# Threshold attention and feed-forward on one core: the last two score tiles of five head pairs take their threshold from a DMA add instead of VectorE

## The chip, the cores and the metric

One Trainium2 chip, one core. The metric is the device time of one execution in microseconds. The engines are named as in the profile: PE is TensorE (PEld its weight loads), DVE is VectorE, ACT is ScalarE, POOL is GpSimd, SP is SyncE. Every engine takes its instructions from its own queue in order and waits on semaphores; SP, ACT and POOL also issue DMAs.

## The reference

```python
# q, k, v: (8, 8, 576, 64) float32; tau scalar; w_in (512, 2048), w_out (2048, 512)
scores = scale * np.matmul(q, k.transpose(0, 1, 3, 2))
thresh = np.max(scores, axis=-1, keepdims=True) - tau
scores = np.where(scores >= thresh, scores, -1000000000.0)
scores = scores - np.max(scores, axis=-1, keepdims=True)
attn = np.exp(scores)
attn = attn / (np.sum(attn, axis=-1, keepdims=True) + 1e-09)
attn_out = np.matmul(attn, v)
x = attn_out.transpose(0, 2, 1, 3).reshape(4608, 512)
h = x @ w_in
out = (h * (1.0 / (1.0 + np.exp(-1.702 * h)))) @ w_out
```

## The kernel before, in words

The heads are worked in 32 pairs, four pairs (numbers 0 to 3) being the first batch. A pair's scores are held transposed, keys on partitions: `scores` makes nine groups of 64 keys of both heads (four matmuls each, two trace instructions per float32 matmul), and `keep` (ACT, L588) copies each group from PSUM into SBUF. Two groups form a tile of 128x1152; there are four such tiles and a short one of 128x576, numbered t = 0 to 4.

The threshold of a query is the maximum over keys less tau. DVE reduces each tile (`in_groups`, L594) and then over tiles (`over_tiles`, L603); ACT crosses the partition halves (`cross_max`, L613) and DVE joins them (`over_halves`, L620). For the pairs in `BY_DMA` (1, 3, 4, 5, 6) the result is turned (`turn_rows`, L627), written to a row in DRAM (`row_out`, L643) and read back over all partitions into a tile `mb` (`row_in`, L652), both issued on POOL. The others spread it by a DVE transpose (`spread_max`, L631). Then, tile by tile, DVE subtracts the threshold (`sub`, L658), ACT multiplies what is negative by a steep factor (`mask`, L664) and takes the exponential (`exps`, L668). PE multiplies by the values (L679, `pv`) and, for pairs 0 to 3, by ones for the sums (L679, `den`); `place_x` (L783) scales the product into the feed-forward input.

The weights arrive as 32 pieces that ACT and DVE convert: `cv_power` (L494), `cv_power2` (L498) and `cv_round` (L512) on ACT, `cv_low`, `cv_whole` and `cv_end` (L526) on DVE. The first two feed-forward blocks are plain: `mm1_0` (L838), `tanh`, `gelu_0`, then `mm2` (L820). The later blocks use seven products in place of eight (`product1`, L908; `product`, L1230), for which sums of weight quarters are made by accumulating DMAs on POOL (`t_plus`, L954; `w_plus`, L877). From pair 6 on, the scores of a pair are interleaved on PE with the products of an earlier one.

The order of all this is fixed when the program is built. Each step is a `task` with an engine, a planned cost and a rank; the tables `EARLY` (pairs 0 to 3), `SECOND` (4 to 7), `LATER`, `CV`, `W_RANK` and `L_RANK` are offsets to the ranks. `run_in_order` plays the planned costs, and on each engine emits the ready task of lowest rank. So a change of one cost or rank can change the order on every engine. A `transfer` stands for a DMA in that plan.

Of the kernel before, what the change touches and what calls it, by code (L numbers as in the profile page):

```python
# [17 lines left out]
ALU = mybir.AluOpType  # L18
# [14 lines left out]
def kernel(  # L33
# [81 lines left out]
    flat = [const.tile([P, 32], FP32, name=f"flat{j}") for j in range(2)]  # L115
# [15 lines left out]
    for x in ("raw0", "raw1", "qkT0", "qkT1", "mb"):  # L131
# [3 lines left out]


    EARLY = {
        "cross_max": -48.44,
        "exps": 8.27,
        "in_groups": -20.58,  # L140
        "keep": -91.91,
        "load_qk": -140.68,
        "load_v": -22.28,
        "mask": 10.76,
        "one_row": -86.85,
        "over_halves": -24.87,
        "over_tiles": -88.47,
        "place_x": -38.02,
        "row_in": 3.21,
        "row_out": -7.31,  # L150
        "scores_run": -131.23,
        "spread_max": 29.73,
        "spread_sums": 7.58,
        "sub": -0.95,
        "sums_by_pe": 0.48,
        "turn_in": -85.72,
        "turn_rows": -3.66,
        "turned": -73.29,
        "values": 4.21,
    }  # L160
    SECOND = {
        "cross_max": 21.33,
        "cross_sums": 28.0,
        "exps": -7.59,
        "in_groups": 89.35,
        "keep": 7.69,
        "load_qk": -3.13,
        "load_v": 156.87,
        "mask": 62.12,
        "over_halves": -25.79,  # L170
        "over_tiles": 12.47,
        "place_x": -6.25,
        "prep": 141.1,
        "row_in": 11.9,
        "row_out": 159.53,
        "scores_run": -65.52,
        "spread_max": 4.94,
        "sub": 100.98,
        "sums_in": 1.57,
        "sums_out": 102.83,  # L180
        "turn_rows": -12.68,
        "turn_sums": -7.39,
        "values": -29.52,
    }
    LATER = {
        "cross_max": 26.13,
# [17 lines left out]
        "values": 4.3,  # L204
    }
    CV = {
        "cv_end": 0.86,
        "cv_low": 87.73,
        "cv_power": 34.31,
        "cv_power2": 17.48,  # L210
        "cv_round": -2.96,
        "cv_whole": 74.25,
        "load_w": -29.8,
    }

    LAG = {"PE": 0.26, "DVE": 0.18, "ACT": 0.22, "POOL": 0.18, "SP": 0.1}
# [5 lines left out]
    def task(engine, cost, rank, f, *a, after=(), take=(), give=(), lag=None):  # L222
        if lag is None:
            lag = LAG[engine]
        if rank != FIRST and rank < LAST and f not in (first_act, tau_terms, run_up, stay_warm):
            biases = EARLY if a[0] < NPAIR else SECOND if a[0] < 2 * NPAIR else LATER
            rank += CV[f.__name__] if f.__name__ in CV else biases.get(f.__name__, 0.0)
        tasks.append((engine, cost, rank, f, a, [x for x in after if x is not None],
                      take, give, lag))
        return len(tasks) - 1  # L230
# [9 lines left out]
    def transfer(by, time, a, kind=0, give=(), lag=1.7):  # L240
        return task(by, time, FIRST, moved, kind, after=[a], give=give, lag=lag)
# [102 lines left out]
    BY_POOL = {}  # L344
# [63 lines left out]
    def own(n, *pools):  # L408
        return tuple(x + "_apart" for x in pools) if n in APART else pools
# [122 lines left out]
    mats, sT, stats, mbs, rows, pss = {}, {}, {}, {}, {}, {}  # L532
# [92 lines left out]
    def turn_rows(n):  # L625

        nc.vector.transpose(out=flat[1], in_=flat[0])  # L627

    def spread_max(n):
        mb = home(n, "mb")  # L630
# [16 lines left out]

    def row_in(n):
        mb = home(n, "mb")
        row = rows.pop(n)  # L650
        for c in range(2):
            row_queue(n).dma_start(out=mb[ts(c, KT)], in_=row[c : c + 1].to_broadcast([KT, S]))  # L652
        mbs[n] = mb

    def sub(n, t):
        s = sT[n, t].rearrange("p u h s -> p u (h s)")
        engine = nc.gpsimd if t in BY_POOL.get(n, ()) else nc.vector
        engine.tensor_tensor(  # L658
            out=s, in0=s, in1=mbs[n].unsqueeze(1).to_broadcast(list(s.shape)), op=ALU.subtract
        )  # L660

    def mask(n, t):
# [607 lines left out]
    for x in other:  # L1270
# [4 lines left out]
        out=eye, in_=eye, compare_op=ALU.not_equal, fill=1.0, base=0, pattern=[[-1, P]],  # L1275
# [3 lines left out]
        out=tau_b, in_=bass.AP(tensor=tau.tensor, offset=tau.offset, ap=[[0, P], [1, 1]])  # L1279
# [36 lines left out]


    SUMS_BY_PE = (0, 1, 2, 3)
    BY_DMA = (1, *range(3, SINGLE))
    SUMS_BY_DMA = range(4, NP)  # L1320
    LEAD = 6
# [4 lines left out]
    FFU = 1.727  # L1326
    T_RANK = FIRST

    W_RANK = (-72.29, -7.42, 1.49, 46.38, 3.78, 10.04)
    W_TIME = 1.8  # L1330
    WARM = 22
    ROUND_BY_ACT = range(n_in)
# [2 lines left out]
    for i in range(len(pieces)):  # L1335
        y = 0 if i < NDC else 2 if i < n_in else 4
        n = NDC if i < NDC else n_in - NDC if i < n_in else n_in
# [28 lines left out]
    placed, spread, ffn = {}, {}, []  # L1366
# [478 lines left out]
            next_blk += 1  # L1845

    crossed = {"max": [], "sums": []}
    L_RANK = (-39.87, -74.91, 155.66, -21.93, -34.74, 174.67, -5.56, -9.93, 5.49, 3.95, 23.52, -15.1, 43.37, 150.16, 100.05, 1.56, -41.98, 6.75, 20.12, -0.89, 1.38, 148.42, -40.7, -50.66)

    def load_rank(n, which):  # L1850
        return L_RANK[3 * n + which] if 3 * n < len(L_RANK) else 0.0
# [16 lines left out]
    for n in range(NP):  # L1868
        gate = per_pair * (n - LEAD)
        assert gate < len(ffn) or gate <= 0  # L1870
        after = [ffn[gate]] if gate >= 0 and ffn else []
        r = float(n)

        slow = 1.1 if n < 2 * NPAIR else 1.0
        rq = ("POOL", 1.4, "DMW", 2.2) if n in ROWS_BY_POOL else ("SP", 1.0, "DMS", 1.7)
        flow = 2.9 if n in (0, 1, 4) else 0.0
        by_sp = n not in ROWS_BY_POOL
# [31 lines left out]
        mx, copies = [], []  # L1909
# [18 lines left out]
        if n >= JOINT:  # L1928

            a = None  # L1930
            for t in range(NKT + 1):
                js = range(2 * t, min(2 * t + 2, NK))
                m = ahead(n)
                w = task(
                    "PE", 0.485 * len(js), r, values, m, [t],
                    after=exped[m] + [loaded[m], pq, pk] + after if t == 0 else [a],
# [6 lines left out]
                a = w  # L1943
                for j in js:
                    w = task(
                        "PE", 0.485, r, scores_run, n, [j], after=[a], take=("psA",),
                        give=own(n, "qkT0", "qkT1") if j == NK - 1 else (),
# [3 lines left out]
                    a = w  # L1951
                if t == NKT:
                    valued(m, w)
        else:
            for js in [range(x, x + 3) for x in range(0, NK, 3)] if n >= WHOLE else [[x] for x in range(NK)]:
# [3 lines left out]
                a = task(  # L1959
                    "PE", 0.484 * slow * len(js), r, scores_run, n, js, after=[pq, pk] + after,  # L1960
                    take=("psA",) * len(js) + new,
                    give=own(n, "qkT0", "qkT1") if js[-1] == NK - 1 else (),
                )
                after = [a]
                for j in js:
                    copied(n, r, j, a)
        a = task("DVE", 0.41, r, over_tiles, n, ALU.max, after=mx)
        quick = n in BY_DMA
        a = task(
            "ACT", 0.45 if quick else 0.85, r, cross_max, n, after=[a, tau_done] + crossed["max"],  # L1970
        )
        a = task("DVE", 0.24, r, over_halves, n, after=[a], take=("row",) if quick else ())
        crossed["max"] = [a]
        if n in BY_DMA:
            a = task("DVE", 0.14, r, turn_rows, n, after=[a])
            a = transfer(rq[2], 0.3 + 0.4 * by_sp, task(rq[0], 0.65 * rq[1], r, row_out, n, after=[a]), lag=1.7 - 0.4 * by_sp + flow)
            spread[n] = task(rq[0], 1.1 * rq[1], r, row_in, n, after=[a], take=own(n, "mb"))
            m = transfer(rq[2], 1.1, spread[n], 0 if by_sp else 1, give=("row",), lag=rq[3] + flow)
        else:
            m = task("DVE", 0.78, r, spread_max, n, after=[a], take=own(n, "mb"))  # L1980
        spread.setdefault(n, m)
        ws, subs = [], [(m, None)]
        for t in range(NKT + 1):
            tail = t == NKT
            pool = t in BY_POOL.get(n, ())
            a = task(
                "POOL" if pool else "DVE", (1.45 if pool else 0.68) if tail else 2.7 if pool else 1.3,
                r, sub, n, t, after=[y for y, x in subs if tail or x in (None, pool)],
                give=own(n, "mb") if tail else (),
            )  # L1990
            subs.append((a, pool))
            a = task("ACT", 0.58 if tail else 1.08, r, mask, n, t, after=[a])
            ws.append(task("ACT", 0.77 if tail else 1.25, r, exps, n, t, after=[a]))
        loaded[n] = lv
# [87 lines left out]
```

## Time and profile before

| | us |
|---|---|
| median of 3 runs | 1248.26 (1247.51 to 1250.88) |
| the profiled execution | 1251.82 |
| its span, first to last instruction | 1250.0 |
| outside the span | 1.8 |
| PE busy | 1222.6 (98%) |
| DVE busy | 1085.7 (87%) |
| ACT busy | 827.7 (66%) |
| POOL busy | 32.6 (3%) |

A group line of the profile gives line, engine, operation, output and input with their shapes, the count, then busy time in us and the mean length of one in ns, and last the idle time of the engine just before them with what ended it. A line of the order in time gives start and length in us, and in brackets the idle time before it. Line numbers are those of the kernel before.

### The profile page before, as it was taken

The page shows a single profiled execution, that of the slowest core. Times are in us where ns is not written, and L with a number is a line of the kernel's source. Part 1 is how long each engine was busy: PE and PEld are TensorE (multiplying, and loading weights), DVE is VectorE, ACT ScalarE, POOL GpSimd, SP SyncE. Part 2 cuts the span into 40 slices and gives each one's busy share as a digit, 9 for nine tenths or more (in the row PEclk, how much of TensorE's full clock was granted, in tenths as well). Part 3 has the DMA queues.
Part 4 walks back from the last instruction along what each step waited for, and adds up shares of the span by engine and source line. Part 5 has one row for each costly group of instructions (what it writes and reads, how often), then busy time and mean ns, then how long its engine had stood idle before and what let it go on. Part 6 is the DMA issues. An engine that isn't in the chain of part 4 may idle for free.

```text
span 1250.0 us, 27210 instructions
## 1 busy us (share of the span) xinstructions
PE 1222.6 (98%) x11264; PEld 1005.3 (80%) x11264; DVE 1085.7 (87%) x1683; ACT 827.7 (66%) x1209; POOL 32.6 (3%) x59
## 2 busy tenths in 40 slices
PE   8979999999999999999999999999999999999998
PEld 6636854487888888887979788888888897999998
DVE  6989997779879998999898998989788789999796
ACT  6999988786766766676767667667667586330430
POOL 0000012110000000000000000000000000000000
PEclk9999999999999999999999999999999999999999
DMA  8724458781313332223323241422221212344443
GB/s 244 189 68 112 140 126 140 145 152 43 72 39 97 68 91 66 79 65 74 92 57 99 46 116 42 116 49 66 44 71 22 64 45 72 114 120 140 144 121 100
DMA packets 187180, 117.05 MB, mean 94 GB/s; under 512 B 145392, under 2 KB 155632, under 8 KB 186928
## 3 DMA queue, kind: packets, MB, share of 16 engines
q1 hardware_dynamic: 179776, 103.93, 31.6%
q0 software_dynamic: 6592, 11.09, 5.1%
q8 instruction: 88, 1.44, 0.5%
q10 hardware_dynamic: 688, 0.30, 0.1%
q14 instruction: 36, 0.29, 0.1%
HBM read 86.28 MB, written 20.60 MB: 85 GB/s over the span
## 4 chain that ended last, share of the span: by engine, by line
PE 74%; DVE 12%; ACT 10%; DMA 3%; issue 1%; POOL 0%; SPq 0%; DVEq 0%; ACTq 0%; POOLq 0%
PE ops L1230 24%; PE hps L908 14%; PE ps L908 10%; PE pv L679 9%; PE ps L571 9%; ACT arena L668 3%; PE hps L1074 3%; DVE arena L1091 2%; ACT arena L664 2%; ACT arena L588 2%; PE ps L1074 2%; PE ps L1191 2%; DVE arena L1149 2%; PE ops L1191 1%; DVE part L594 1%
## 5 line engine op out<-in xcount | busy, mean ns | idle before, releaser
L594 DVE TRANSPOSE_TENSOR_REDUCE part<-arena 128x36 f32<-128x1152 f32 x300 | 365.8, 1242 | 62.4 <-ACT arena L588 50.0
L588 ACT COPY arena<-ps 128x576 f32<-128x576 f32 x288 | 170.6, 642 | 93.3 <-PE ps L571 93.2
L664 ACT ACTIVATE arena<-arena 128x1152 f32<-128x1152 f32 (+1 forms) x160 | 165.8, 1060 | 56.9 <-DVE arena L658 56.9
L668 ACT ACTIVATE arena<-arena,shift,scl 128x1152 f32<-128x1152 f32 (+1 forms) x160 | 196.6, 1247 | 1.9
L658 DVE TENSOR_TENSOR arena<-arena 128x1152 f32<-128x1152 f32 (+1 forms) x158 | 189.2, 1228 | 1.2 <-DMA arena<-row 0.3
L571 PE MATMUL ps<-arena 64*64 64x288 f32 x2304 | 171.5, 409 | 6.2 <-ACT arena L588 6.1
L1230 PE MATMUL ops<-w_out,arena 128*128 128x256 f32 x768 | 175.8, 382 | 0.0
L1230 PEld LDWEIGHTS ops<-w_out,arena 128*128 128x128 f32 x768 | 143.3, 190 | 27.3 <-issue 9.2
L679 PE MATMUL pv<-arena 64*64 64x288 f32 x2176 | 159.2, 405 | 0.0
L571 PEld LDWEIGHTS ps<-arena 64*64 64x64 f32 x2304 | 83.1, 133 | 66.9 <-ACT arena L588 25.7
L1230 PE MATMUL ops<-arena 128*128 128x256 f32 x576 | 128.5, 379 | 0.0
L679 PEld LDWEIGHTS pv<-arena 64*64 64x64 f32 x2176 | 80.8, 133 | 53.5 <-issue 7.7
L1230 PEld LDWEIGHTS ops<-arena 128*128 128x128 f32 x576 | 109.3, 190 | 15.3 <-issue 0.4
L908 PE MATMUL hps<-xT,w_in 128*128 128x128 f32 x768 | 89.7, 275 | 0.0
L908 PEld LDWEIGHTS hps<-xT,w_in 128*128 128x128 f32 x768 | 88.6, 192 | 1.1 <-issue 0.5
L927 DVE TENSOR_TENSOR arena<-ps,arena 128x512 f32<-128x512 f32 x72 | 46.9, 679 | 44.0 <-PE ps L908 41.3
L922 ACT COPY arena<-hps 128x512 f32<-128x512 f32 x72 | 41.4, 575 | 39.4 <-PE hps L908 39.3
L838 PE MATMUL hps<-xT,w_in 128*128 128x256 f32 x256 | 56.1, 380 | 0.0
L820 PE MATMUL ops<-w_out,arena 128*128 128x512 f32 x128 | 55.9, 595 | 0.0
L838 PEld LDWEIGHTS hps<-xT,w_in 128*128 128x128 f32 x256 | 48.4, 190 | 7.8 <-issue 0.9
L1088 ACT COPY arena<-hps 128x512 f32<-128x512 f32 x38 | 22.2, 583 | 47.7 <-PE hps L1074 47.7
L613 ACT ACTIVATE other<-red,minus_gap 32x18 f32<-32x18 f32 x118 | 36.2, 307 | 25.0 <-DVE red L603 23.4
(211 smaller groups left out, 1773.3 us busy)
## 6 DMA issues: line engine op xcount, KB each, us to landing
arena<-in_v_dram SPq DMA_DIRECT2D x128, 144.0 KB
arena<-exu SPq DMA_DIRECT2D x42, 256.0 KB
arena<-ext SPq DMA_DIRECT2D x39, 256.0 KB
out_dram<-osb SPq DMA_DIRECT2D x32, 256.0 KB
arena<-in_q_dram SPq DMA_DIRECT2D x112, 72.0 KB
arena<-in_k_dram SPq DMA_DIRECT2D x112, 72.0 KB
arena<-row_s SPq DMA_DIRECT2D x48, 144.0 KB
w_out<-in_moe_w_in_dram SPq DMA_DIRECT2D x12, 512.0 KB
```

The costliest lines, as they stand in the source:

```text
L571: nc.tensor.matmul(ps[ts(c, KT), h, 0:SH], lhsT=mats[n, 1][ts(h, D), ts(j, KT)], rhs=mats[n, 0][ts(h, D), ts(c, SH)], start=True, stop=True,)
L588: nc.scalar.copy(out=sT[n, t][:, u], in_=pss.pop((n, j))[:, :, 0:SH])
L594: nc.vector.tensor_reduce(out=stats[n, op][:, t * 2 * QB : min(2 * t + 2, NK) * QB], in_=sT[n, t].rearrange("p u h (g d) -> p (u h g) d", ...
L658: engine.tensor_tensor(out=s, in0=s, in1=mbs[n].unsqueeze(1).to_broadcast(list(s.shape)), op=ALU.subtract)
L664: nc.scalar.activation(out=s, in_=s, func=AF.Prelu, alpha=STEEP)
L668: nc.scalar.activation(out=s, in_=s, func=AF.Exp, scale=scl, bias=shift)
L679: nc.tensor.matmul(o[c][ts(h, D), 0:SH], lhsT=left(j, h)[ts(c, KT)], rhs=sT[n, t][ts(c, KT), u, h, :], start=(j == 0), stop=(j == NK - 1),)
L820: nc.tensor.matmul(acc[i], lhsT=g0[:, j, ts(i, P)], rhs=w_out[:, j, :], start=(j == 0), stop=(j == NFC - 1),)
L838: nc.tensor.matmul(hidden[j][:, ts(i, BLK)], lhsT=w_in[:, c, ts(j, P)], rhs=xTs[i][:, c, :], start=(c == 0), stop=(c == NDC - 1),)
L908: nc.tensor.matmul(o[:, ts(j, HT)], lhsT=left[:, c, ts(4 * y + j, P)], rhs=right[:, c, :], start=(x in (P1, P2, P5) and j + c == 0), stop= ...
L1074: nc.tensor.matmul(o[:, ts(j, HT)], lhsT=left[:, ts(j, P)], rhs=right, start=(m in (P1, P2, P5) and j == 0), stop=(j == 3), skip_group_che ...
L1230: nc.tensor.matmul(banks[blk][k][:, ts(o, HM)], lhsT=left[:, j, :], rhs=right[:, j, :], start=(j == 0), stop=(j == HF - 1),)
```

## The change

For pairs 1, 3, 4, 5 and 6 the threshold row is written with its sign turned, and DVE's `sub` becomes an addition. Tiles 3 and 4 of these pairs are no longer touched by DVE: two DMAs per tile, issued on POOL, add the DRAM row to the scores in SBUF, 64 partitions each. Tiles 0 to 2 stay with DVE. The mask of tiles 3 and 4 waits for those transfers. All rank tables but `LATER` have new numbers, which change the order on every engine up to the first seven-product block.

```diff
     EARLY = {
+        "add_row": -17.09,
         ...
     SECOND = {
+        "add_row": 200.86,
         ...
     def turn_rows(n):
         nc.vector.transpose(out=flat[1], in_=flat[0])
+        nc.vector.tensor_single_scalar(out=flat[1], in_=flat[1], scalar=-1.0, op=ALU.mult)
 
     def row_in(n):
         mb = home(n, "mb")
-        row = rows.pop(n)
+        row = rows[n]
         ...
+    def add_row(n, t):
+        s = sT[n, t].rearrange("p u h s -> p u (h s)")
+        for c in range(2):
+            nc.gpsimd.dma_start(
+                out=s[ts(c, KT)],
+                in_=rows[n][c : c + 1].unsqueeze(1).to_broadcast([KT, s.shape[1], S]),
+                accum_op=ALU.add,
+            )
 
     def sub(n, t):
         ...
         engine.tensor_tensor(
-            out=s, in0=s, in1=mbs[n].unsqueeze(1).to_broadcast(list(s.shape)), op=ALU.subtract
+            out=s, in0=s, in1=mbs[n].unsqueeze(1).to_broadcast(list(s.shape)),
+            op=ALU.add if n in BY_DMA else ALU.subtract,
         )
 
+    ADDED = {n: (3, 4) for n in (1, *range(3, 7))}
     BY_DMA = (1, *range(3, SINGLE))
 
-    W_RANK = (-72.29, -7.42, 1.49, 46.38, 3.78, 10.04)
+    W_RANK = (21.78, -2.79, 5.54, 197.74, -5.69, 18.68)
 
         for t in range(NKT + 1):
             tail = t == NKT
             ...
+            if t in mine:
+                last_add = task("POOL", 1.3, r, add_row, n, t, after=[last_add] + copies)
+                a = transfer(
+                    "DMW", 2.0 if tail else 4.0, last_add, 1, lag=2.0, give=("row",) if t == mine[-1] else (),
+                )
+            else:
+                a = task(
+                    "DVE", 0.68 if tail else 1.3, r, sub, n, t, after=[y for y, _ in subs],
+                    give=own(n, "mb") if t == max(set(range(NKT + 1)) - set(mine)) else (),
+                )
+                subs.append((a, None))
             a = task("ACT", 0.58 if tail else 1.08, r, mask, n, t, after=[a])
             ws.append(task("ACT", 0.77 if tail else 1.25, r, exps, n, t, after=[a]))
```

More of the change, by code (lines that the diff above doesn't have):

```diff
@@ L137 @@
     EARLY = {
[L138 to L159, printed above, removed]
+        "add_row": -17.09,
+        "cross_max": -8.9,
+        "exps": 3.4,
+        "in_groups": 40.2,
+        "keep": -1.5,
+        "load_qk": -91.58,
+        "load_v": -17.92,
+        "mask": 20.21,
+        "one_row": -2.23,
+        "over_halves": -1.58,
+        "over_tiles": 12.45,
+        "place_x": 8.65,
+        "row_in": 9.78,
+        "row_out": 16.22,
+        "scores_run": -26.02,
@@ L160 @@
+        "spread_max": 165.03,
+        "spread_sums": 10.43,
+        "sub": -10.09,
+        "sums_by_pe": 145.93,
+        "turn_in": 144.65,
+        "turn_rows": -16.63,
+        "turned": 9.39,
+        "values": 9.14,
     }
     SECOND = {
[L162 to L183, printed above, removed]
+        "add_row": 200.86,
+        "cross_max": 14.92,
+        "cross_sums": -3.76,
+        "exps": 196.61,
+        "in_groups": 45.17,
+        "keep": 10.97,
+        "load_qk": -6.25,
@@ L184 @@
+        "load_v": 11.75,
+        "mask": 208.96,
+        "over_halves": 27.17,
+        "over_tiles": 209.11,
+        "place_x": -2.12,
+        "prep": 3.31,
+        "row_in": 12.82,
+        "row_out": -1.45,
+        "scores_run": 20.0,
+        "spread_max": 28.37,
+        "sub": 205.09,
+        "sums_in": -21.93,
+        "sums_out": 7.71,
+        "turn_rows": 3.91,
+        "turn_sums": 195.63,
+        "values": 199.02,
     }
@@ L206 @@
     CV = {
[L207 to L213, printed above, removed]
+        "cv_end": 11.37,
+        "cv_low": 20.27,
+        "cv_power": 154.74,
+        "cv_power2": 145.18,
+        "cv_round": 95.61,
+        "cv_whole": -5.71,
+        "load_w": -13.29,
     }
@@ L1847 @@
     crossed = {"max": [], "sums": []}
-    L_RANK = (-39.87, -74.91, 155.66, -21.93, -34.74, 174.67, -5.56, -9.93, 5.49, 3.95, 23.52, -15.1, 43.37, 150.16, 100.05, 1.56, -41.98, 6.75, 20.12, -0.89, 1.38, 148.42, -40.7, -50.66)
+    L_RANK = (-86.91, -25.75, 128.47, 8.22, -2.48, 11.0, 12.27, -102.31, 172.12, 213.22, 70.0, 16.64, -8.1, 151.74, 160.47, 136.73, 12.26, 16.28, -17.83, 26.24, 17.55, 17.28, 3.52, 17.34)
     def load_rank(n, which):
@@ L1974 @@
         if n in BY_DMA:
-            a = task("DVE", 0.14, r, turn_rows, n, after=[a])
+            a = task("DVE", 0.22, r, turn_rows, n, after=[a])
             a = transfer(rq[2], 0.3 + 0.4 * by_sp, task(rq[0], 0.65 * rq[1], r, row_out, n, after=[a]), lag=1.7 - 0.4 * by_sp + flow)
             spread[n] = task(rq[0], 1.1 * rq[1], r, row_in, n, after=[a], take=own(n, "mb"))
-            m = transfer(rq[2], 1.1, spread[n], 0 if by_sp else 1, give=("row",), lag=rq[3] + flow)
+            m = transfer(rq[2], 1.1, spread[n], 0 if by_sp else 1, give=() if n in ADDED else ("row",), lag=rq[3] + flow)
         else:
@@ L1981 @@
         spread.setdefault(n, m)
-        ws, subs = [], [(m, None)]
+        ws, subs, last_add = [], [(m, None)], spread[n]
+        mine = ADDED.get(n, ())
         for t in range(NKT + 1):
             tail = t == NKT
[L1985 to L1991, printed above, removed]
+            if t in mine:
[9 more added lines that the diff above has]
+                subs.append((a, None))
             a = task("ACT", 0.58 if tail else 1.08, r, mask, n, t, after=[a])
```

## The prediction

> **What bounds the kernel now.** I read the page first, then stretches of the span, then each engine's instructions in order of time.
>
> ```profile
> span 1250.0 us, 27210 instructions
> PE 1222.6 (98%) x11264; PEld 1005.3 (80%) x11264; DVE 1085.7 (87%) x1683; ACT 827.7 (66%) x1209; POOL 32.6 (3%) x59
> ```
> ```profile
> core 0: us, PE busy (x) PEld busy (x) DVE busy (x) ACT busy (x) POOL busy (x), PEclk, DMA share, GB/s
> 20.00:110.00 90.00, 76.21 (x1147) 46.03 (x1140) 80.16 (x117) 88.44 (x122) 6.29 (x12) 1.00 0.52 140
> 112.71:256.37 143.66, 141.40 (x885) 89.35 (x882) 125.86 (x186) 120.89 (x170) 21.40 (x30) 1.00 0.65 142
> 256.37:1250.00 993.63, 986.01 (x8985) 855.48 (x8983) 866.83 (x1363) 605.39 (x897) 3.10 (x2) 1.00 0.31 80
> ```
>
> The columns are the stretch, its length, then each engine's busy time. From 20 to 110 us ACT is busy 88.4 of 90 us and PE 76.2: the first batch's pairs are bound by ACT. From 112.71 on PE is nearly without a gap. So DVE, which the change relieves, ends last in neither stage.
>
> The two built kernels compared in instruction order add the decisive fact: PE has the same instructions in both, and from the first seven-product block (L908) to the end in the same order. That block begins at 256.37 here; the 993.6 us behind it should stay. What changes is how early PE reaches it, and before it PE's path is:
>
> ```profile
> 109.65 1.99 PE L838 MATMUL hps<-xT,w_in 128*128 128x256 f32 x8
> 112.71 50.34 PE L838 MATMUL hps<-xT,w_in 128*128 128x256 f32 x232
> 167.92 1.26 PE L571 MATMUL ps<-arena 64*64 64x288 f32 x16 [1.80 <-ACT arena L588]
> 177.54 17.33 PE L820 MATMUL ops<-w_out,arena 128*128 128x512 f32 x40
> 194.80 4.60 PE L679 MATMUL pv<-arena 64*64 64x288 f32 x72
> 244.81 1.26 PE L571 MATMUL ps<-arena 64*64 64x288 f32 x16 [0.43 <-ACT arena L588]
> 256.37 3.73 PE L908 MATMUL hps<-xT,w_in 128*128 128x128 f32 x32
> ```
>
> Each line is start, length, work, count and, in brackets, the idle time before it. The first feed-forward matmuls start at 109.65, and run in a row from 112.71 with 8 of 256 done: worth a start in a row at 112.71 − 8 × 50.34/232 = 110.97. After that only 1.80 and 0.43 us are idle. The time can therefore change by (a) this start and (b) waits between it and L908.
>
> **(a) The start: ACT's work ahead of it.** The start follows pair 3's last exponential. From the two orders I counted ACT's instructions up to it. Masks and exponentials are the same; the new order has 4 more `keep`, 2 more `cv_power`, 3 more `cv_power2`, 2 more `cross_max` copies, 3 fewer `cv_round`. Their prices:
>
> ```profile
> L588 ACT COPY arena<-ps 128x576 f32<-128x576 f32 x52 | 30.2, 644 | 4.0 <-PE ps L571 3.9
> L512 ACT ACTIVATE w_out<-w_out,full 128x512 int32<-128x512 f32 x12 | 9.5, 808 | 0.0
> L498 ACT ACTIVATE w_in<-w_in,rebias 128x512 int32<-128x512 f32 x7 | 5.1, 724 | 0.1
> L613 ACT ACTIVATE other<-red,minus_gap 32x18 f32<-32x18 f32 x14 | 4.3, 307 | 0.2
> L494 ACT ACTIVATE w_in<-w_out,rebias 128x512 f32<-128x512 int16 x5 | 4.0, 794 | 0.0
> ```
>
> Busy time over count: 4 × 0.58 + 2 × 0.80 + 3 × 0.73 + 2 × 0.31 − 3 × 0.79 = +4.4 us, all on the path since ACT is full. Against it stands one gap:
>
> ```profile
> 20.61 1.25 ACT L588 COPY arena<-ps 128x576 f32<-128x576 f32 x2 [3.04 <-PE ps L571]
> 17.07 2.23 PE L549 MATMUL ps<-eye,arena 64*64 64x64 f32 x32 [2.72 <-DMA arena<-in_k_dram]
> ```
>
> PE stands on pair 2's keys here, with pair 1's scores queued behind them, and ACT waits for those scores. The new order puts all of pair 1's scores ahead of pair 2's transposes, so I take the 3.04 us as gone (bounds 0 and 3.04). Pair 3 ends 4.4 − 3.0 = 1.4 us later.
>
> Behind that exponential comes a chain:
>
> ```profile
> 102.12 0.87 ACT L668 ACTIVATE arena<-arena,shift,scl 128x576 f32<-128x576 f32 x1
> 104.52 0.66 PE L679 MATMUL den<-arena,ones 64*64 64x288 f32 x8
> 107.52 0.95 DVE L783 TENSOR_TENSOR xT<-pv,arena 128x256 f32<-128x256 f32 x4
> 109.02 1.72 ACT L588 COPY arena<-ps 128x576 f32<-128x576 f32 x3
> ```
>
> The exponential ends at 102.99; its sums start 1.53 us later because PE still has three earlier groups, and x is placed at 108.47. In the new order ACT has two more `keep` and two `cross_max` copies (1.8 us) between the last full exponential and the short one, so PE is through those groups and some 1.3 us of the 1.53 go. Placement comes at 108.47 + 1.4 − 1.3 = 108.6. Before the feed-forward matmuls only three groups of pair 5's scores are left behind pair 3's products, not seven; the third waits for ACT's third `keep` after the exponential: 0.80 + 2 × 0.58 + 0.73 + 0.79 + 0.58 = 4.1 us after 104.4, 108.5, and takes half a microsecond. Start at about 109.1 against 110.97: **−1.9 us** (−4 if the ACT prices, which overlap by some 0.1 us, are high; +3 if the 3.04 us come back elsewhere with more).
>
> **(b) After the start.** The interleaved group of pair 4's products and pair 6's scores stood behind 240 of 256 matmuls of L838 and now stands behind 136: the 1.80 us wait, where ACT had conversions queued ahead of the `keep`s, should go, and so should the 0.43. That is −2.2 us. Against it: at its new place PE arrives at 109.1 + 136 × 0.217 = 138.6, and ACT's work counted from pair 3's end to pair 4's last exponential is some 32 us by the rows above, 104.4 + 32 = 136.4, a margin of 2 us. Pair 5's products, behind 40 matmuls of L820 before, now stand behind 20, 17.33/2 = 8.7 us earlier. I charge +1.5 for new waits (0 to 5).
>
> **What the change adds and takes away by itself.**
>
> ```profile
> L658 DVE TENSOR_TENSOR arena<-arena 128x1152 f32<-128x1152 f32 x16 | 20.9, 1336 | 0.0
> L658 DVE TENSOR_TENSOR arena<-arena 128x576 f32<-128x576 f32 x2 | 1.4, 715 | 0.0
> L594 DVE TRANSPOSE_TENSOR_REDUCE part<-arena 128x36 f32<-128x1152 f32 x23 | 30.6, 1357 | 6.6 <-ACT arena L588 6.5
> L526 DVE SCALAR_TENSOR_TENSOR w_in<-w_out,w_in 128x512 int32<-128x512 int32 x4 | 2.9, 720 | 0.8 <-ACT w_in L498 0.6 <-ACT w_out L512 0.2
> L627 DVE STREAM_TRANSPOSE flat<-flat 128x32 f32<-128x32 f32 x3 | 0.6, 212 | 0.1
> ```
>
> DVE loses 5 × (1.34 + 0.72) = 10.3 us and gains five sign changes of a 128x32 tile, about 1 us (an estimate from the 0.21 of the last row). Of that 2 × 2.06 = 4.1 us lie before pair 3's placement, and the order puts two more group maxima (2 × 1.36) and two more `cv_end` (2 × 0.72) there, with three sign changes: no net relief at the start. The rest falls where PE is full. I count it at nothing.
>
> The additions: 20 issues on POOL and 5 × 864 KB of transfers. No add from a DRAM row is in this trace. The nearest rows are the row's own spread and the accumulating 1 MB adds of the weights:
>
> ```profile
> arena<-w_out POOLq DMA_DIRECT2D x3, 1024.0 KB, 9.9
> arena<-row POOLq DMA_DIRECT2D x10, 144.0 KB, 4.7
> 81.30 1.07 POOL L652 DMA_DIRECT2D arena<-row  x2 [1.08 <-DMA row<-flat]
> 184.90 1.65 POOL L954 DMA_DIRECT2D arena<-w_out  x1 [4.00 <-ACT arena L950]
> 77.17 0.62 ACT L613 ACTIVATE other<-red,minus_gap 32x18 f32<-32x18 f32 x2
> 90.04 1.17 ACT L664 ACTIVATE arena<-arena 128x1152 f32<-128x1152 f32 x1
> ```
>
> Between those ends, 4.7 and 9.9 us, I take 8 for a tile of 576 KB, nearer the accumulating row. Pair 3 is the tight case. ACT's work between its `cross_max` and its first mask is 12.6 us by the same prices, as it was (77.79 to 90.04). So on this clock the adds are issued behind 82.4, the large tile's two by 82.4 + 2 × 1.65 = 85.7, and landed by 95.6 at the worst row. ACT wants that tile after three masks and exponentials and two `keep`: 90.04 + 3 × 2.5 + 1.2 = 98.7. Hidden, with 3 us or more to spare. The new wait stands in ACT's queue: behind it are the exponential, two `keep`, and PE's sums. On POOL, the next pair's row, pair 4's sums and the weights' adds now queue behind these issues; POOL is 3% busy, which hides 20 issues of 0.5 to 1.65 us. For pairs 4 to 6 the adds stand in the stretch where PE has feed-forward matmuls to do; lateness there is part of the 0 to 5 of (b). Pair 1's adds are followed by most of pair 1's and pair 2's ACT work and are hidden the same way.
>
> **Sum**: −1.9 − 2.2 + 1.5 = −2.6 us. The profiled execution (1251.82, span 1250.0) would become 1249.2, span 1247.4; taken off the median 1248.26, which lies 3.6 below that execution: **1245.7 us**. About 0.3%, 3.7 us, is what a measurement here can tell from no change.
>
> **Rivals.**
> 1. *Adds land late (slower).* Place: ACT's mask of pair 3's fourth tile. It decides once a large tile lands over 13 us after its issue (85.7 to 98.7). For: 64 partitions read one DRAM row, which no accumulating row here does. Against: 1 MB takes 9.9. At 20 us ACT stands 7 us, and with −2.6 the result is +4.4, 1252.7; 1254 at 21.3 us. Chance 0.15.
> 2. *Descriptor writing is shut out by DVE.* The row: POOL's issues keep 0.5 us per DMA with DVE busy 80 of 90 us. If each of four issues waited out a 1.34 us DVE operation, the adds would come 5.4 us later, past the margin by 2.3: −0.3, or up to +4 if the other pairs pay as much, 1252. Chance 0.04. The Trainium skill, page "SBUF — State Buffer", section "SBUF: two separate sides", states this: while VectorE runs a two-port operation, GpSimd can't write the descriptors of its own DMAs. By that rule the adds are the wrong place for this work; the trace's steady 1.07 us for two issues shows no sign of it.
> 3. *Weights first.* Five more weight pieces are queued ahead of pair 2's second query half. If it lands late, ACT stands at the copy of pair 2's queries and the 3.04 us return: +0.4, or +4 with new waits at their bound. Chance 0.10.
> 4. *The gain is eaten* by waits at their bound between 109 and 256 us: −1 to +3, about 1248.5. Chance 0.15.
> 5. *More comes*, the low ends of (a) and (b): −4 − 2.2 + 0 = −6 and a little beyond, 1242. Chance 0.12.
>
> **How the numbers follow.** My case, −1 to −5.5, has 0.44, half of it beyond 3.7 us. Faster: 0.22 + 0.12 = 0.34. Slower: all of rival 1, 0.05 of 3, 0.03 of 2, 0.02 of 4: 0.25. Within 0.3%: 0.41. The range is 1241 (rival 5's low end) to 1254 (rival 1); my case alone is 1243 to 1247.
>
> **What would show it.** L908 should begin near 253.8, the first matmul of L838 near 109, ACT's 3.04 us gap at 17 to 21 us and PE's 1.80 should be gone, and no mask should wait for a DMA for over 0.5 us. I am wrong in mechanism if masks wait on `row` transfers by several microseconds, or if L838 starts after 112.

## The result, and the profile after

| | before | after |
|---|---|---|
| median, us | 1250.32 (1247.51 to 1253.43, 12 runs) | 1248.47 (1247.18 to 1249.01, 12 runs) |
| ratio of after to before | | 0.9984, 95% interval 0.9976 to 0.9992 |
| profiled execution, its span, us | 1251.82, 1250.0 | 1248.48, 1246.6 |

The changed kernel is 1.9 us faster, 0.16%, which is within the 0.3% that was set as "no change". The forecast was 1245.7. The three runs of the kernel before that were known then had the median 1248.26; twelve have 1250.32, and 22 to 33 runs beside the later experiments 1250.0 to 1250.4.

The page after has these shares. Against the lines of before, DVE is 8.7 us less busy and POOL 19.3 us more; ACT is the same.

```profile
span 1246.6 us, 27241 instructions
PE 1220.6 (98%) x11264; PEld 1004.2 (81%) x11264; DVE 1077.0 (86%) x1678; ACT 827.7 (66%) x1209; POOL 51.9 (4%) x79
```

Line numbers are those of each kernel. In the changed one, `keep` is L590, `mask` L677, `exps` L681, `sub` L670, `add_row` L661, `mm1_0` L851, `gelu_0` L857 and `product1` L921. PE in order of time (start, length, work, count, idle time before it and what ended it):

```profile
17.69 2.57 PE L573 MATMUL ps<-arena 64*64 64x288 f32 x24 [2.09 <-ACT arena L563]
...
93.89 2.20 PE L692 MATMUL den<-arena,ones 64*64 64x288 f32 x16 [4.72 <-ACT arena L681]
...
109.75 21.02 PE L851 MATMUL hps<-xT,w_in 128*128 128x256 f32 x96
131.07 8.90 PE L851 MATMUL hps<-xT,w_in 128*128 128x256 f32 x40 [0.30 <-DVE arena L857]
...
253.27 3.73 PE L921 MATMUL hps<-xT,w_in 128*128 128x128 f32 x32
```

The feed-forward matmuls run in a row from 109.75, where the kernel before was worth 110.97. The waits of 1.80 and 0.43 us behind them are gone, and one of 0.30 is new. The first seven-product block begins at 253.27, not 256.37. Two stretches of the span, in the columns used before, the second from that block to the end:

```profile
20.00:109.75 89.75, 76.06 (x1180) 47.59 (x1176) 78.21 (x117) 88.51 (x124) 13.54 (x20) 0.97 0.60 150
253.27:1246.60 993.33, 986.11 (x8985) 855.54 (x8983) 868.67 (x1368) 605.69 (x898) 3.10 (x2) 1.00 0.31 80
```

The stretch behind the block takes 993.33 us (993.63 before). So the start of that block is a finer measure than the total, with one caution: it is read from a single execution, which in the experiments lay up to 2.1 us off its kernel's median (1251.74 against 1249.60), and the execution of before lay 1.5 us above its own. By medians the gain is 1.9 us, not the 3.1 between the two starts.

### The profile page after: what moved, and what is told of

Its sections match the earlier page's. It is cut to its first block, busy times and chain, and to the rows that moved or that the text cites. A ratio compares the mean times of both kernels' runs of the same rounds, so it can differ in the third digit from the quotient of the medians.

```text
span 1246.6 us, 27241 instructions
## 1 busy us (share of the span) xinstructions
PE 1220.6 (98%) x11264; PEld 1004.2 (81%) x11264; DVE 1077.0 (86%) x1678; ACT 827.7 (66%) x1209; POOL 51.9 (4%) x79
## 4 chain that ended last, share of the span: by engine, by line
PE 80%; DVE 9%; ACT 7%; issue 2%; DMA 1%; SPq 0%; ACTq 0%; DVEq 0%
PE ops L1243 24%; PE hps L921 14%; PE ps L921 10%; PE pv L692 10%; PE ps L573 9%; PE ops L833 4%; PE hps L1087 3%; DVE arena L1104 2%; ACT arena L681 2%; PE ps L1087 2%; PE ps L1204 2%; ACT arena L677 2%; DVE arena L1162 2%; PE ops L1204 1%; ACT arena L590 1%
## 5 line engine op out<-in xcount | busy, mean ns | idle before, releaser
L596 DVE TRANSPOSE_TENSOR_REDUCE part<-arena 128x36 f32<-128x1152 f32 x300 | 366.3, 1243 | 64.2 <-ACT arena L590 49.9
L590 ACT COPY arena<-ps 128x576 f32<-128x576 f32 x288 | 170.6, 641 | 93.2 <-PE ps L573 92.7
L677 ACT ACTIVATE arena<-arena 128x1152 f32<-128x1152 f32 (+1 forms) x160 | 165.9, 1059 | 55.5 <-DVE arena L670 55.4
L681 ACT ACTIVATE arena<-arena,shift,scl 128x1152 f32<-128x1152 f32 (+1 forms) x160 | 196.6, 1247 | 1.8
L670 DVE TENSOR_TENSOR arena<-arena 128x1152 f32<-128x1152 f32 (+1 forms) x150 | 180.3, 1236 | 0.9
L921 PE MATMUL hps<-xT,w_in 128*128 128x128 f32 x768 | 89.6, 275 | 0.0
L921 PEld LDWEIGHTS hps<-xT,w_in 128*128 128x128 f32 x768 | 88.6, 192 | 1.0 <-issue 0.5
L851 PE MATMUL hps<-xT,w_in 128*128 128x256 f32 x256 | 56.3, 381 | 0.3 <-DVE arena L857 0.3
L851 PEld LDWEIGHTS hps<-xT,w_in 128*128 128x128 f32 x256 | 48.1, 190 | 8.6 <-DVE arena L857 1.4
```

What stands on the lines that cost most here:

```text
L590: nc.scalar.copy(out=sT[n, t][:, u], in_=pss.pop((n, j))[:, :, 0:SH])
L596: nc.vector.tensor_reduce(out=stats[n, op][:, t * 2 * QB : min(2 * t + 2, NK) * QB], in_=sT[n, t].rearrange("p u h (g d) -> p (u h g) d", ...
L670: engine.tensor_tensor(out=s, in0=s, in1=mbs[n].unsqueeze(1).to_broadcast(list(s.shape)), op=ALU.add if n in BY_DMA else ALU.subtract,)
L677: nc.scalar.activation(out=s, in_=s, func=AF.Prelu, alpha=STEEP)
L681: nc.scalar.activation(out=s, in_=s, func=AF.Exp, scale=scl, bias=shift)
L851: nc.tensor.matmul(hidden[j][:, ts(i, BLK)], lhsT=w_in[:, c, ts(j, P)], rhs=xTs[i][:, c, :], start=(c == 0), stop=(c == NDC - 1),)
```

## The experiments

What each version took, as the ratio to the kernel before (95% interval) beside its median. "Keys late" is one move in the old order, explained at its run.

| order | DMA adds for pairs | us | ratio |
|---|---|---|---|
| old | all five | 1251.47 | 1.0011 (1.0001 to 1.0020) |
| new | none | 1253.86 | 1.0032 (1.0021 to 1.0043) |
| new | 1, 3 | 1252.42 | 1.0021 (1.0012 to 1.0029) |
| new | 4, 5, 6 | 1250.17 | 0.9998 (0.9989 to 1.0007) |
| new | 1, 3, 4, 5 | 1248.87 | 0.9990 (0.9981 to 0.9999) |
| new | all five: the changed kernel | 1248.47 | 0.9984 (0.9976 to 0.9992) |
| new | all five, each add twice | 1263.30 | 1.0101 (1.0087 to 1.0115) |
| old, keys late | none | 1247.81 | 0.9981 (0.9972 to 0.9991) |
| old, keys late | 4 | 1246.92 | 0.9971 (0.9960 to 0.9983) |
| old, keys late | 4, 5 | 1248.84 | 0.9988 (0.9979 to 0.9997) |
| old, keys late | 4, 5, 6 | 1249.60 | 0.9999 (0.9990 to 1.0008) |
| old, keys late | all five | 1250.37 | 1.0004 (0.9994 to 1.0013) |

### The adds alone, in the order of before

```diff
     def row_in(n):
     ...
+        for t in (3, 4):
+            ...
+            for c in range(2):
+                nc.gpsimd.dma_start(
+                    out=s[ts(c, KT)],
+                    ...
+                    accum_op=ALU.add,
+                )
     def sub(n, t):
+        if n in BY_DMA and t >= 3:
+            return
         ...
```

The sign of the row and the operation of `sub` change as in the changed kernel. The adds are issued directly behind the row's spread.

> The old instruction order on PE, ACT and SP, with tiles 3 and 4 of pairs 1 and 3 to 6 taken from DVE and added by DMAs issued right behind the row's spread. Theory A (the new order is the cause, DVE's relief is worth nothing): the first L908-type product starts within 1 us of 256.4, the time is within 0.1% of before; pair 6's adds are the only ones near their masks (issued about 191 to 194, wanted from 205) and may cost up to 2 us. Theory B (DVE's relief of 10 us is the cause): the product starts at 253 to 254.5 and the time falls by 0.15 to 0.3%.

Measured: 1251.47 us, ratio 1.0011. PE's lines (`keep` is L588, the block L919):

```profile
165.62 1.26 PE L571 MATMUL ps<-arena 64*64 64x288 f32 x16 [0.48 <-ACT arena L588]
...
254.65 3.73 PE L919 MATMUL hps<-xT,w_in 128*128 128x128 f32 x32
```

The wait of 1.80 us has shrunk to 0.48 and the block begins between the places that the two theories gave, and yet there is no gain in the medians: this execution (1250.14) lies 1.3 us below its own. The time is nearer to theory A: in the old order the adds of all five pairs do not pay.

### The order alone, VectorE doing the work

```diff
     def add_row(n, t):
+        return
         ...
     def sub(n, t):
+        for x in (2, 3, 4) if n in ADDED and t == 2 else (t,):
         ...
```

The plan still counts the adds, so the order is the new one; DVE adds the row to tiles 3 and 4 directly behind tile 2.

> The new instruction order on PE, ACT and SP, with DVE doing the additions of tiles 3 and 4 directly behind tile 2's, and no adds by DMA. Theory A: DVE had idle time ahead of the start of the feed-forward block (6.3 and 6.4 of 10 us busy in two slices before 110), so the first seven-block product starts at 253 to 255 and the time stays 0.1 to 0.2% under before. Theory B: 4 us come back before pair 3's placement and 10 us in all, the product starts at 256 or later and the time is that of before or above.

Measured: 1253.86 us, 1.0032, slower than before. PE (`gelu_0` is L858, `mm1_0` L852):

```profile
110.13 17.53 PE L852 MATMUL hps<-xT,w_in 128*128 128x256 f32 x80
129.36 3.72 PE L852 MATMUL hps<-xT,w_in 128*128 128x256 f32 x16 [1.69 <-DVE arena L858]
...
175.62 3.72 PE L852 MATMUL hps<-xT,w_in 128*128 128x256 f32 x16 [1.75 <-DVE arena L858]
...
257.55 3.73 PE L922 MATMUL hps<-xT,w_in 128*128 128x128 f32 x32
```

The start, 110.13, is only 0.4 us later than that of the changed kernel. What is lost comes behind it: PE waits for gelu. DVE's own queue just before the first of these waits shows why, here

```profile
122.34 0.69 DVE L858 SCALAR_TENSOR_TENSOR arena<-th,hps 128x512 f32<-128x512 f32 x1
...
123.55 3.29 DVE L671 TENSOR_TENSOR arena<-arena 128x1152 f32<-128x1152 f32 x3
...
128.66 0.65 DVE L858 SCALAR_TENSOR_TENSOR arena<-th,hps 128x512 f32<-128x512 f32 x1
```

and in the changed kernel:

```profile
121.97 0.69 DVE L857 SCALAR_TENSOR_TENSOR arena<-th,hps 128x512 f32<-128x512 f32 x1
...
123.18 1.35 DVE L670 TENSOR_TENSOR arena<-arena 128x1152 f32<-128x1152 f32 x1
...
126.35 0.65 DVE L857 SCALAR_TENSOR_TENSOR arena<-th,hps 128x512 f32<-128x512 f32 x1
```

Between two gelus stand three subtractions instead of one (3.29 against 1.35), and the second gelu starts 2.3 us later. The adds therefore bring 1253.86 − 1248.47 = 5.4 us in the new order, and the new order without them costs 3.5. Both figures hold for subtractions that stand directly behind tile 2's, three in a row; the new order with each of them in a place of its own was not run. My theory that the new order made the gain and DVE's relief nothing has fallen.

### Which pairs' adds pay, in the new order

```diff
+    ADD_PAIRS = (4, 5, 6)        # second run: (1, 3); third run: (1, 3, 4, 5)
     ...
     def add_row(n, t):
+        if n not in ADD_PAIRS:
+            return
         ...
     def sub(n, t):
+        for x in (2, 3, 4) if n in ADDED and n not in ADD_PAIRS and t == 2 else (t,):
         ...
```

> The new order with the DMA adds kept for pairs 4 to 6 alone; for pairs 1 and 3 VectorE adds the row to tiles 3 and 4 itself, straight behind tile 2. Theory (the relief pays only between 110 and 180 us, where VectorE is full beside the feed-forward blocks): the first seven-product block begins at 253 to 254, as with all adds (253.27), the time stays 1.5 to 2.5 us under the kernel before, and the waits of 1.69 and 1.75 us on gelu, which the new order has without any adds, are gone. Rival (the relief of pairs 1 and 3 counts, because the start of the feed-forward blocks hangs on it): the first feed-forward block starts 1 us or more later and the block begins at 255.5 or later, the time being level with the kernel before. A half-way result, 254.3 to 255.5, would say that both halves of the relief count.

> The converse: the new order with the DMA adds kept for pairs 1 and 3 alone; VectorE does tiles 3 and 4 of pairs 4 to 6. Theory (relief pays only between 110 and 180 us): the start of the first feed-forward block is as with all adds (109.7 to 110.2), but PE waits for gelu again, 3 to 4 us in all between 110 and 180, the first seven-product block begins at 256.5 to 257.5 and the time is 2.5 to 3.5 us over the kernel before. Rival (pairs 1 and 3 matter): the block begins at 254.5 or earlier.

> The changed kernel without pair 6's adds (VectorE does them): pair 6's subtractions lie behind 180 us, where VectorE is busy 47 of 70 us. Theory (relief pays only where VectorE is full, 110 to 180): same time as the changed kernel, 1248 to 1249, first seven-product block at 253 to 253.8. Rival (pair 6's relief counts): 1249.5 or more.

Measured: 1250.17, 1252.42 and 1248.87 us. PE with pairs 4 to 6:

```profile
110.94 21.02 PE L853 MATMUL hps<-xT,w_in 128*128 128x256 f32 x96
132.24 9.00 PE L853 MATMUL hps<-xT,w_in 128*128 128x256 f32 x40 [0.28 <-DVE arena L859]
...
254.81 3.73 PE L923 MATMUL hps<-xT,w_in 128*128 128x128 f32 x32
```

and with pairs 1 and 3:

```profile
111.21 17.53 PE L853 MATMUL hps<-xT,w_in 128*128 128x256 f32 x80
130.44 3.72 PE L853 MATMUL hps<-xT,w_in 128*128 128x256 f32 x16 [1.69 <-DVE arena L859]
...
176.63 3.72 PE L853 MATMUL hps<-xT,w_in 128*128 128x256 f32 x16 [1.74 <-DVE arena L859]
...
258.44 3.73 PE L923 MATMUL hps<-xT,w_in 128*128 128x128 f32 x32
```

The gelu waits go with the adds of pairs 4 to 6 and stay without them, as the theory says; those adds bring 3.7 us (from 1253.86). But the block begins at 254.81, the half-way result, and the time is level with the kernel before: by the medians pairs 1 and 3 count as well, 1.4 us (1253.86 to 1252.42) or 1.7 (1250.17 to 1248.47). The two agree in sign, but in both the intervals of the ratios overlap, so the size is uncertain. The place is not shown. The theory gave a start of 109.7 to 110.2 with the adds of pairs 1 and 3; it came at 111.21, later than with no adds (110.13), and the block at 258.44, not at 256.5 to 257.5. These are single executions, and a part of their differences is PE's clock (see the last section). Without pair 6's adds the block begins at 253.71 and the time is that of the changed kernel within 0.4 us: behind 180 us, where DVE is not full, the adds bring nothing that can be measured.

### Each add twice

```diff
     def add_row(n, t):
         ...
-        for c in range(2):
+        for c in (0, 1, 0, 1):
```

Tiles 3 and 4 then hold other values. The second add to a tile also waits for the first to land (52.7 us of such waits on POOL in all), so it costs more than the transfers alone.

> The changed kernel with each add issued twice (the row is added two times, so tiles 3 and 4 of these pairs hold other values). Theory A (adds hidden with some 7 us to spare): pair 3's fourth tile lands about 97 to 99.5 where ACT wants it at 99.7, so the first seven-block product moves by 0 to 1.5 us from 253.3. Late adds (rival 1 of the prediction): ACT's masks of tiles 3 and 4 wait for DMAs and the product moves by 5 us or more.

Measured: 1263.30 us, and the block begins at 269.32, 16 us later than in the changed kernel: the second theory's outcome. First PE's lines, then the one wait of over 5 us in ACT's:

```profile
110.21 21.03 PE L851 MATMUL hps<-xT,w_in 128*128 128x256 f32 x96
...
142.85 3.68 PE L851 MATMUL hps<-xT,w_in 128*128 128x256 f32 x8 [4.17 <-DVE arena L857]
...
224.72 1.24 PE L573 MATMUL ps<-arena 64*64 64x288 f32 x8 [5.66 <-DVE red L752]
```

```profile
138.61 0.68 ACT L677 ACTIVATE arena<-arena 128x576 f32<-128x576 f32 x1 [5.16 <-DMA arena<-row]
```

But it is not at rival 1's place: pair 3's fourth tile bears even the doubled adds, and the start is at 110.21. What comes late is pair 4's short tile (ACT stands 5.16 us, then PE 4.17), and the sums of a later pair, whose row goes over the same POOL queue (5.66).

### One move in the old order: pair 2's keys behind pair 1's scores

```diff
+                if f in (turn_in, turned) and a == (2, 1):
+                    held_back.append((f, a))
+                    continue
                 ...
+                if f is scores_run and a[0] == 1 and list(a[1]) == [NK - 1]:
+                    for f, a in held_back:
+                        f(*a)
```

> The old kernel and order with one move: pair 2's key transposes and their copy stand behind all of pair 1's scores instead of ahead of them. By the prediction's term: ACT's gap of 3.04 us at 17.6 to 20.6 goes, pair 3's last exponential ends near 100 instead of 103.0, the first seven-block product starts at 253 to 254.5, the time falls by 0.15 to 0.25%. Rival: the gap was not on the path, ACT waits for pair 0's or pair 1's maxima instead, and the product starts within 0.7 us of 256.4.

Measured: 1247.81 us, 0.9981, as fast as the whole change, with no DMA add. PE (`mm1_0` is L845; of its 256 matmuls 8 come ahead of the row, as in the kernel before):

```profile
110.83 50.34 PE L845 MATMUL hps<-xT,w_in 128*128 128x256 f32 x232
166.05 1.26 PE L578 MATMUL ps<-arena 64*64 64x288 f32 x16 [1.80 <-ACT arena L595]
...
253.91 3.73 PE L915 MATMUL hps<-xT,w_in 128*128 128x128 f32 x32
```

and ACT a little before that wait, where a conversion stands for a piece of the weights:

```profile
163.03 0.77 ACT L501 ACTIVATE w_out<-arena,rebias 128x512 f32<-128x512 int16 x1 [1.97 <-DMA arena<-in_moe_w_out_dram]
```

The row starts 1.88 us earlier than before (112.71). The step "ACT's 3.04 us gap is on the path" is shown, with 1.9 to 2.5 us of it coming through. The 1.80 us wait is untouched, and so is ACT's wait for the weights ahead of it, 1.98 us in the kernel before.

### The move and the adds together, in the old order

```diff
+    ADD_PAIRS = (4, 5, 6)        # others: all five; (4, 5); (4,)
     ...
```

The adds are issued directly behind the row's spread, as in the run with the adds alone.

> The kernel before with two edits: pair 2's key transposes behind pair 1's last scores (as in the run with that move alone, 1247.81) and the DMA adds for pairs 4 to 6 alone, in the old order. Theory (DVE relief pays where DVE is full and PE waits): PE's wait of 1.80 us at the interleaved group behind 240 matmuls shrinks to 0.5, as it did with all adds in the old order, while nothing is added early; the first seven-product block begins at 252.5 and the time is 1246.5, under both kernels. Rival (in the old order that wait is ACT's own queue and the adds bring nothing, or their POOL issues hold up pair sums): 253.9 and 1247.8, as without adds, or later.

> As the run before this one, but with the DMA adds for all five pairs (1 and 3 to 6). If the adds of pairs 1 and 3 bring nothing where ACT is the bound, it equals the one with pairs 4 to 6 (1246.5). If they cost there (the old order with all adds and without the move was 1.1 us slower than the kernel before), it is 1 to 2.5 us above that one, 1247.5 to 1249. If they help the start, the first feed-forward block starts earlier by up to 2 us and the time is about 1245.

> The old order, pair 2's key transposes late, DMA adds for pairs 4 and 5 only. With adds for pair 6 too, PE stood 2.98 us at 212.05 for pair 5's sums, whose row's transfers were queued on POOL behind pair 6's four adds. Theory (that queue is the cause): without pair 6's adds this wait is under 0.5 us, the 1.80 us wait at 166 stays away, the first seven-product block begins at 251.5 to 252.5 in a like execution and the median is 1246 to 1247, the best of all. Rival (any add on POOL in this stretch delays the sums, or the wait has another cause): the wait stays at 2 us or more and the median is 1248.5 to 1250.

> The same with pair 4's adds alone. If VectorE's relief by pair 4 is what lets the weight transfer land sooner that ACT waited 1.97 us for at 163, the 1.80 us wait of PE is gone here too and the median is 1246 to 1247; if it is pair 5's relief, the wait is still there and the time is that of the move alone (1247.8).

Measured: 1249.60, 1250.37, 1248.84 and 1246.92 us. With pairs 4 to 6 the theory failed on the total. PE (`mm1_0` is L857, the block L927), DVE and POOL in that kernel:

```profile
212.05 0.71 PE L578 MATMUL ps<-arena 64*64 64x288 f32 x8 [2.98 <-DVE red L758]
...
256.06 3.73 PE L927 MATMUL hps<-xT,w_in 128*128 128x128 f32 x32
```

```profile
210.95 0.95 DVE L802 TENSOR_TENSOR xT<-pv,arena 128x192 f32<-128x192 f32 x4 [1.28 <-DMA arena<-row_s]
```

```profile
185.12 4.45 POOL L666 DMA_DIRECT2D arena<-row  x4
...
197.25 1.64 POOL L973 DMA_DIRECT2D arena<-w_out  x1 [1.46 <-ACT arena L969]
202.58 1.25 POOL L774 DMA_DIRECT2D arena<-row_s  x2 [3.69 <-DMA row_s<-flat_s]
```

The 1.80 us wait is gone, but pair 6's four adds (185.12) and a weight add (197.25) go over the queue that carries pair 5's sums. Their row is read back only at 202.58, lands after 210 us, and PE stands 2.98 us. With the adds of all five pairs PE stands 1.48 us at the same place, and the median is 0.8 us higher, the intervals overlapping: those of pairs 1 and 3 do not help here, and whether they cost is not settled. Without pair 6's adds (pairs 4 and 5) the wait is gone: the theory of the queue holds for it. Its median does not: 1248.84 was in the rival's range, and the block begins at 253.41, not at 251.5 to 252.5. A smaller wait has come. POOL and then PE of that kernel, with pairs 4 and 5:

```profile
168.93 1.23 POOL L774 DMA_DIRECT2D arena<-row_s  x2 [3.16 <-issue]
...
182.23 1.63 POOL L973 DMA_DIRECT2D arena<-w_out  x1 [5.23 <-ACT arena L969]
```

```profile
211.55 1.26 PE L578 MATMUL ps<-arena 64*64 64x288 f32 x16 [0.99 <-ACT arena L595]
...
253.41 3.73 PE L927 MATMUL hps<-xT,w_in 128*128 128x128 f32 x32
```

and of the kernel with pair 4's adds alone:

```profile
166.40 1.21 POOL L774 DMA_DIRECT2D arena<-row_s  x2 [1.62 <-issue]
...
180.05 1.63 POOL L973 DMA_DIRECT2D arena<-w_out  x1 [3.99 <-ACT arena L969]
```

```profile
109.53 50.34 PE L857 MATMUL hps<-xT,w_in 128*128 128x256 f32 x232
168.75 3.72 PE L857 MATMUL hps<-xT,w_in 128*128 128x256 f32 x16
...
250.97 3.73 PE L927 MATMUL hps<-xT,w_in 128*128 128x128 f32 x32
```

With pair 4 alone the sums are read back 2.5 us earlier and the weight add is issued 2.2 us earlier. PE then has no wait left between 109.53 and 168.75 that the trace lists, and the block begins at 250.97. So it is pair 4's relief that takes the 1.80 us away. ACT's wait of 1.97 us for a piece of the weights is gone as well (the conversion runs at 159.67 without a wait); why the piece is there sooner is not shown. Not all of the 2.9 us between this block and that of the move alone (253.91) are pair 4's: 1.3 of them are there at 64 us, before its adds are issued at 105.60, and the medians differ by 0.9. The 0.99 us wait with pair 5's adds stands behind work that is 2.2 to 2.5 us late in the lines above; that the delayed sums are its cause is read from the order of these lines, not isolated. At 1246.92 (1246.38 to 1247.81) this version is the fastest of all, 0.9971, ahead of the move alone (0.9981) and the changed kernel (0.9984), though its interval overlaps with both.

## Why the prediction was right on the outcome and wrong on the source

**The fixed stretch.** Right: 993.33 against 993.63 us, and 993.4 to 993.9 in the experiments (span less the block's start).

**(a) The start.** Forecast 109.1, measured 109.75; the term of −1.9 came out as −1.2. ACT's gap of 3.04 went, and the old order with that one move shows that it was on the path. But the new order has early waits of its own (PE's 2.09 at 17.69, ACT's 2.82 at 9.60 where 0.91 stood before): the waits that the trace lists for ACT ahead of pair 3's last exponential fell from 8.9 to 6.9 us, by 2.1 and not by 3.0. The mask of pair 3's fourth tile and that last exponential:

```profile
99.67 1.18 ACT L677 ACTIVATE arena<-arena 128x1152 f32<-128x1152 f32 x1
...
104.68 0.87 ACT L681 ACTIVATE arena<-arena,shift,scl 128x576 f32<-128x576 f32 x1
```

It ends at 105.55, 1.2 us after the 104.4 forecast; the tail behind it is 4.2 us where 4.7 was counted. The size was off, not the path, and about 1.0 of the 1.2 us is this gap.

**(b) Behind the start.** The 1.80 and 0.43 us went, as said. One cause was missed: the conversion ahead of the `keep`s stood itself 1.98 us for its piece of the weights (at 164.91 in the kernel before). New waits were charged at 1.5 us; all that is left is 0.30 plus small change, since 253.27 − 109.75 = 143.5 us stand against 145.4 before. That is −1.9 against the −0.7 forecast.

**DVE's relief "at nothing": the step that failed.** It was worth 5.4 us in this order. I looked for DVE's cost only ahead of the start, and from "PE is full behind it" concluded that DVE could not matter there. But PE was full because DVE's gelu came just in time: in the changed kernel the gelu of 126.35 ends at 127.00, and PE, with 80 matmuls behind it, needs it at 109.75 + 17.53 = 127.28. In the new order, with more subtractions ahead of it, PE waits for a gelu twice by 1.7 us. The small total was the sum of two larger terms that I had not seen: +3.5 for the order, −5.4 for the adds. I compared the new order with the adds in it and called what came out the order's. That path came nearly as I described it only because the adds kept gelu in time, which I did not know; that the total came near is to this extent luck.

**The adds hidden.** Right for the changed kernel: no mask waits for a DMA. The trace's lines for the add's issues and landings:

```profile
L661 POOL DMA_DIRECT2D arena<-row x20: 1047/1554/2107, 42.0 to 185.9; - x20
DMA to landing us min/median/max: 4.5/7.1/9.5
```

The landing of 8 us was a fair guess between 4.7 and 9.9. The record of one issue lasts up to 2.1 us where 1.65 was the bound, but the records overlap: the four of a pair take 3.74 (below), 0.94 each. Pair 3's adds are all issued by 87.50, landed by 97.0 at the longest time, and ACT's mask starts at 99.67: 2.7 us to spare. "POOL is 3% busy, which hides 20 issues" was too easy. Its busy time is small, but the transfers queued on it are not, and in the old order, with pair 6's adds among them, they held up pair sums by 1.5 to 3 us of PE's time.

**Rivals.** Adds late (1) did not happen. Weights first (3) did not return as an ACT gap at pair 2's queries. The measured 1248.47 is the number of rival 4 and lies outside the 1243 to 1247 of my own case, but not for rival 4's reason, since only 0.30 us of new waits came; the reason is the 3.6 us that were taken off at the end (see the number, below). Against the median of twelve runs the change is −1.9, inside my case's −1 to −5.5. More (5) did not come. For rival 2, two stretches in which POOL issues a pair's four adds (columns as before):

```profile
83.76:87.50 3.74, 3.74 (x64) 2.15 (x57) 2.17 (x3) 3.71 (x7) 3.74 (x5) 1.00 0.77 164
110.16:113.95 3.79, 3.79 (x19) 3.33 (x18) 3.79 (x5) 3.76 (x7) 3.79 (x5) 1.00 0.94 206
```

DVE is busy 2.17 of 3.74 us in the first and all of 3.79 in the second, and the issues take the same time. Nothing was shut out. Most of DVE's work in the second is this line:

```profile
111.27 3.26 DVE L596 TRANSPOSE_TENSOR_REDUCE part<-arena 128x36 f32<-128x1152 f32 x3
```

The rule cited with rival 2 had a second half that I left out: the Trainium skill, page "SBUF — State Buffer", section "Who interferes with whom", names copies, casts and `tensor_scalar` as the operations that can take both ports, and says that `tensor_reduce` never contends with GpSimd on trn2. So by the page the rule does not reach the reductions of these stretches, and its first half is not tested by them. Between 132.70 and 136.45 two `TENSOR_SCALAR` of 0.44 us on DVE (L521) stand beside pair 5's adds, and the four issues take 3.75 us; whether those two took both ports no run shows.

**The number.** The changed kernel's profiled execution was forecast at 1249.2 and came at 1248.48. The 1245.7 came from taking off 3.6 us, the distance of before's profiled execution from a median of three runs. With more runs that distance is 1.5, and the term of 3.6 was mis-sized by 2.1 us.

## What to carry to other kernels

An engine at full use is bound only as long as what feeds it stays in time: before calling another engine's relief worthless, look at how much slack its last producer has (here DVE's gelu, 0.3 us, against 1.35 for one subtraction). When an edit and a new order come together, run each without the other, since two terms of opposite sign may hide in a small total. Moving work from an engine to a DMA queue cost little by itself here, 0.94 us for an issue, but what stands behind it on that queue inherits the transfers. What the adds were worth hung on the order: in the new one all five pairs together brought 5.4 us; in the old one, with the keys late, pair 4's brought 0.9, not clear of the noise, and with those of more pairs the median rose again (1248.84, 1249.60, 1250.37).

## What the runs showed of the hardware that was not expected

After PE's idle 4.72 us the same 16 `den` matmuls took 2.20 us instead of 1.20, and the granted clock of the slice from 90 to 100 us is 0.83:

```profile
90.00:100.00 10.00, 6.11 (x77) 3.42 (x80) 9.43 (x14) 9.90 (x12) 0.00 (x0) 0.83 0.63 136
```

From 94 to 96 us it is 0.50. How long this lasts differs between the traces of the new order: with no adds the slice has 0.83 too, in the other four it has 0.66, as with the adds of pairs 1 and 3:

```profile
90.00:100.00 10.00, 5.70 (x48) 3.03 (x52) 9.65 (x13) 9.57 (x11) 0.00 (x0) 0.66 0.71 142
```

From the start of that `den` group to the feed-forward matmuls it takes 15.86 us in both traces with 0.83 (93.89 to 109.75 in the changed kernel), and 16.10 to 16.91 in the four with 0.66 (94.30 to 111.21 in this one). Here the two groups behind it are slow as well (2.14 and 1.98 us; 1.64 and 1.14 in the changed kernel). So in these traces a longer stretch goes with a start that is 0.2 to 1.05 us later, and a start read from a single execution carries this. The Trainium skill, page "TensorE: Matmul & The Clock Gate", section "Part 1: The HAM clock gate", says that PE's clock is halved after an idle window of about 3.4 us, whose phase is not tied to the kernel. The traces agree in size: 0.17 of 10 us lost at half rate would be 3.4 us, and 0.34 twice that (estimates from the two rows above). They do not settle the cause: in the old order with all adds a `den` group also took 2.20 us after an idle time of only 1.07, and in the kernel before 1.20 after the same 1.07.
